# The same tasks in another order, in a delta-rule kernel followed by a gated feed-forward

## The chip, the core and the metric

The kernel runs on one core of a Trainium2 chip. The metric is the device time of one execution in microseconds (us); lower is better. Five engines of the core work side by side, each through its own instructions in a fixed order: TensorE (PE, matrix multiplication), VectorE (DVE), ScalarE (ACT), GpSimd (POOL) and SyncE (SP, which here only issues DMAs). An engine that comes to an instruction whose inputs are not ready waits, and everything behind it on that engine waits too. So the order of the instructions on each engine is a choice that decides what waits for what.

## The reference

Inputs q, k and v have the shape (4 batches, 8 heads, 768 tokens, 48); beta has one number for each token and head. Each head carries a 48x48 state through its tokens, and the result goes through a feed-forward of 384 to 2048 to 384:

```python
for t in range(S):
    kt, vt, bt = (k_n[:, :, t], v[:, :, t], beta[:, :, t, None])
    y[:, :, t] = np.einsum('bhd,bhde->bhe', q[:, :, t], state)
    v_old = np.einsum('bhde,bhd->bhe', state, kt)
    state = state + bt[:, :, :, None] * np.einsum('bhd,bhe->bhde', kt, vt - v_old)
...
h = x @ w_in          # x: (3072, 384), y with the heads side by side
g = h * np.cos(h)
return (g @ w_out).astype(np.float32)
```

k_n is k divided by its norm.

## The kernel before, in words

**Attention.** The 768 tokens are cut into 24 *units* of 32 tokens (n = 0 to 23); two units are a *pair* (m = 0 to 11). Within a unit the recurrence is solved at once: `turn(n)` and `gram(n)` (PE) make the products of the unit's keys and queries, `gram_keys` and `gram_queries` (DVE) scale and mask them, and `gram_put` and `gram_get` (SP) carry them through DRAM into the layout of the *inverse*. The inverse of pair m, `inv(m, 0)` to `inv(m, 6)` (lines 687 and 694), inverts triangular 32x32 blocks column by column, with a product and a subtraction for each column; it runs on GpSimd, only that of pair 0 (four steps, half size) on VectorE. `put(m)` and `get(n)` (SP) carry the result through DRAM back to where PE reads it as `zt` (`halves_z` in pair 0, with `get_odd(0)` issued on ScalarE's queue).

Then comes the chain from unit to unit: `state(n)` (PE, line 744), `old(n)` (ACT, 756), `right(n)` (DVE, 763), `solve(n)` (PE, 807 and 813; in pair 0 preceded by `solve_half`, `half_out`, `between` and `between_out`), `solve_out(n)` (DVE, 821), `update(n)` (PE, 834), `update_out(n)` (DVE, 842). `within(n)` (PE, 851), `within_out(n)` (ACT, 864) and `features(n)`, `features_out(n)` turn the unit's output into the input of the feed-forward.

**Feed-forward.** It works on pairs p = 0 to 11 of 256 rows. Pairs 0 and 1 use plain matmuls: `hidden(p, f)` (PE, 923), f = 0, 2, ..., 14, each with four steps after it: `turns` (ACT, 961), `rest` (DVE, 968), `cos` (ACT, 977), `gate` (DVE, 986), which together make h cos h. From pair 2 on, `layer(p, i)` (PE, 1105) uses sums of weights (`in_sums`, DVE, 1003 and 1007) and of inputs (`x_sum`, DVE) so that fewer products are needed; its `layer_copy` (ACT, 1121) and `merge` (DVE, 1007) join the pieces. The second matrix, `out(p, ...)` (PE, 1125 for pair 0, 1182 after), uses sums `right` of the weights and `left` of the gates (DVE, 1198) in the same way, and `collect` and `store` bring the result out. Two names are used twice: `right(n)` with one number is attention's, `right(x, e)` with two is a sum of weights.

**Weights.** The two matrices arrive as 64-bit floats and are narrowed on the chip in 28 pieces t: `weights(t)` (a DMA of 512 KB or 384 KB), `split(t)` (ACT, 448 and 450), `shift(t)` (DVE, 454 and 459), `add(t)` (POOL, 463). Pieces 0 to 11 are w_in: `hidden(p, 4)` and `hidden(p, 12)` need adds 0 to 8, `hidden(p, 6)` and `hidden(p, 14)` all of 0 to 11.

**What sets the order.** Each of these steps is a *task*, added with its engine and the tasks it needs. The class `Order` holds a list of numbers, `LINE`, each the number of a task, and `run` emits the tasks in that order. Each engine then executes its own tasks in the order in which they stand in `LINE`; the dependencies between engines become semaphores. Buffers are handed out in the same order too: a task that needs one of the eight large buffers "g" or of the three PSUM banks "h", or the single banks "two" and "kq", gets the one that was freed first, and waits for the last reader of what lay in it. So the order also decides which task's end sets a buffer free for which other task.

```python
for key in line:
    emit, deps, makes, uses = self.tasks[key]
    ...
        if tag in free:
            self.home = homes[t] = free[tag].pop(0)
    emit()
```

Of the kernel before, what the change touches and what calls it, by code (L numbers as in the profile page):

```python
# [53 lines left out]
0 1 2 3 4 5 6 2095 14 10 11 74 38 75 43 12 7 15 39 16 2099 40 44 13 41 45 46 77 48 99 17 47 18 49 19  # L54
20 78 2103 81 100 79 50 2107 102 2100 82 51 80 9 83 107 2111 2101 103 84 52 108 53 135 2108 2096 54
2102 104 55 105 2097 86 2104 2112 56 2115 37 57 109 2116 2119 160 2120 22 138 85 2109 110 42 2117
2098 2113 111 23 2105 2118 2123 2106 21 24 2121 2122 2114 112 25 139 2110 114 2124 140 26 2127 113
2125 2128 27 28 29 8 2131 136 30 31 2135 2129 32 33 142 34 59 141 193 2139 2126 58 143 2143 35 36
2132 2140 144 161 2136 115 60 2133 713 145 2144 76 146 61 62 63 64 2147 65 218 116 117 2148 66 2151
714 718 2141 2130 118 67 719 68 101 715 2137 70 69 2155 2134 164 720 723 119 2145 147 2142 2152 165  # L60
716 166 120 2149 2153 106 137 2138 2159 717 71 194 724 721 167 168 72 722 2156 121 169 2150 196 725
197 726 728 2157 2163 198 2154 2158 122 729 727 73 171 852 170 730 855 2160 2167 88 87 172 162 2171
89 200 733 2164 201 2161 731 738 853 199 90 91 732 856 734 2168 2169 92 2146 2165 735 743 736 737
251 2175 93 95 748 765 96 94 173 97 2170 174 124 2172 123 98 739 740 2179 2173 753 2162 202 741 742
276 859 744 2166 125 749 2183 745 750 203 205 204 126 781 2180 127 2181 746 163 2174 754 253 2176
309 747 786 128 129 175 782 2184 783 857 751 131 2182 2177 2187 254 752 176 132 2185 130 854 784
2188 2178 791 785 792 793 133 134 219 149 794 2189 222 787 177 788 796 2186 2191 334 858 795 223 150
2195 801 224 789 2192 178 2190 790 802 257 769 2193 179 2196 806 803 225 2199 797 2194 227 798 226
2197 148 799 804 755 2203 255 151 2198 2200 800 770 773 805 811 2201 152 2204 228 229 816 774 256
153 2202 258 2205 154 863 156 311 807 155 766 2206 157 756 812 181 195 312 757 808 259 759 180 158  # L70
868 182 809 861 183 869 860 184 864 871 185 280 813 760 220 279 186 159 862 188 814 810 777 865 189
815 761 822 367 762 190 281 187 872 817 221 191 260 261 818 262 207 230 866 763 758 231 819 820 771
772 780 821 232 824 873 282 315 192 778 316 827 208 283 764 828 874 876 875 830 877 285 832 233 886
768 234 888 767 887 825 823 889 826 892 890 235 775 893 252 878 867 879 895 894 901 891 317 833 903
896 284 882 209 834 829 236 902 897 898 899 880 237 263 904 835 911 836 900 905 906 881 907 206 909
313 287 286 885 210 908 779 211 914 910 912 212 288 213 915 913 214 838 215 925 916 289 917 216 239
918 919 338 840 238 831 841 920 240 884 921 392 290 776 922 241 242 923 924 277 217 842 931 243 926
927 244 314 246 932 425 928 929 843 247 245 933 930 934 248 844 291 837 249 935 936 883 845 846 870
940 337 318 941 942 292 937 319 320 310 839 265 943 944 946 848 849 938 945 939 952 250 947 339 293
948 949 850 966 950 951 953 960 340 369 996 965 997 961 341 847 954 962 321 373 342 999 343 955 1008  # L80
998 963 964 294 1009 956 968 957 1012 1000 971 958 1010 959 295 1014 972 1011 278 1013 370 1015 974
967 1016 1001 266 969 970 1025 374 1002 267 1017 1023 976 1018 1003 375 1019 264 1004 344 977 268
1024 1026 296 269 1020 978 1027 1028 851 1033 1007 345 979 1029 973 1021 1022 975 270 1030 272 980
395 1031 982 273 1036 1032 271 297 371 274 1034 450 1037 1035 984 298 346 985 372 1038 986 1039 299
1040 300 1041 983 1047 1042 1043 335 301 1044 302 987 1045 347 304 275 1046 1053 305 348 431 988 981
989 396 336 349 1048 1049 306 1054 1050 1055 307 1005 990 1006 992 483 1051 1052 1056 1062 1057 993
303 308 376 1063 1058 1064 1065 1059 994 1068 1060 1061 1066 377 378 1067 350 427 991 1074 1069 432
397 1087 1121 1075 1076 1118 1070 1090 1077 1078 1071 398 1119 1072 1079 323 1080 1073 1130 1081 995
1132 1082 1093 1083 1120 399 1131 1084 428 1085 1086 368 351 400 1088 1094 1134 1123 352 353 433 429
1136 1096 379 1089 1098 1133 1091 1092 1138 324 1135 1137 1145 1099 325 401 322 1139 453 1146 402  # L90
430 1122 1140 1126 326 1100 1141 1147 1101 1142 1125 1148 1102 327 1104 1143 403 1149 328 1150 1151
508 330 404 1129 1144 1124 393 489 454 331 1153 1154 1155 1152 1158 1106 329 1156 1095 1159 1097
1157 1160 1107 1161 1103 354 1108 1169 1162 355 1163 1109 1110 332 1128 405 1164 1165 1166 455 1167
# [1640 lines left out]
```

## Time and profile before

| what | value |
|---|---|
| median of 3 runs (lowest, highest) | 656.38 us (654.41, 659.73) |
| the profiled execution, its own time | 657.18 us |
| its span, first to last instruction | 655.2 us |
| mean granted TensorE clock in it | 0.990 |
| busy DVE, ACT, POOL in the span | 538.3, 356.6, 359.6 us |
| longest wait of GpSimd for a DMA of `gb` (inverse's input) | 16.4 us |
| longest wait of PE, for the DMA of `halves_z` | 16.5 us |
| DMA bytes | 59.40 MB, mean 91 GB/s |

The span is divided in the page into 40 slices of 16.4 us, with one digit for each engine: its busy share in tenths. In the views by time, a row has the start and the duration in us, the engine, the line, the operation, the tiles it writes and reads, their shape, and how many equal instructions were merged into it; in brackets stands the idle time before it and what ended that.

### The profile page before, as it was taken

Reading aid. Unit: us, or ns where it says so; the run is one execution under the profiler, and the core shown is the slowest. Engines: PE = TensorE matmul, PEld = TensorE weight load, DVE = VectorE, ACT = ScalarE, POOL = GpSimd, SP = SyncE. Lnnn points to the kernel's source line nnn. Section 1 sums busy time; section 2 is a strip of 40 time slices with the busy share of each in tenths; the row PEclk is TensorE's granted clock in tenths of the full one; section 3 lists DMA queues with packets and bytes.
Section 4 is the critical chain, followed back from the end, with each engine's and each line's share of the span. In section 5 each row is a group of like instructions: output and inputs, shape, how many; then the busy total and the mean of one; then the engine's idle time right before and its main releaser. Section 6 shows DMA issues by size and latency. Waiting matters only on the chain.

```text
span 655.2 us, 23573 instructions
## 1 busy us (share of the span) xinstructions
PE 594.3 (91%) x9724; PEld 552.3 (84%) x9724; DVE 538.3 (82%) x1098; ACT 356.6 (54%) x656; POOL 359.6 (55%) x735
## 2 busy tenths in 40 slices
PE   3326799999989999999999999999999999999997
PEld 3216688886788999998998998999999999989997
DVE  5684497979978998989988988989898879688782
ACT  3535386655346565556655565655665566556440
POOL 4258879877847748537718677178088284000000
PEclk9999699999999999999999999999999999999999
DMA  8887575466443554554454633553441513110001
GB/s 153 197 189 160 126 164 137 96 146 94 92 90 66 99 101 82 111 90 66 94 103 81 130 63 69 92 95 72 92 69 51 105 29 79 29 38 25 1 13 37
DMA packets 237070, 59.40 MB, mean 91 GB/s; under 512 B 228516, under 2 KB 231860, under 8 KB 236964
## 3 DMA queue, kind: packets, MB, share of 16 engines
q1 hardware_dynamic: 233956, 57.03, 44.3%
q8 instruction: 77, 1.26, 0.8%
q10 hardware_dynamic: 2752, 0.43, 0.5%
q0 software_dynamic: 256, 0.44, 0.3%
q14 instruction: 29, 0.24, 0.1%
HBM read 43.17 MB, written 14.68 MB: 88 GB/s over the span
## 4 chain that ended last, share of the span: by engine, by line
PE 59%; POOL 10%; DVE 7%; DMA 7%; ACT 7%; issue 5%; SPq 3%; POOLq 0%; ACTq 0%; DVEq 0%
PE p_h L1105 24%; PE p_out L1182 22%; POOL part L687 5%; POOL z L694 4%; ACT y L864 2%; PE p_s L834 2%; PE p_u L813 2%; PE p_g L577 2%; PE p_kq L851 2%; PE p_kq L744 2%; DVE p_h L1007 2%; PE p_o L1182 2%; DMA kp<-in_k_dram 1%; ACT g_ffn L1121 1%; POOL w_out L463 1%
## 5 line engine op out<-in xcount | busy, mean ns | idle before, releaser
L687 POOL TENSOR_TENSOR part<-z,gb 128x126 f32<-128x126 f32 (+22 forms) x341 | 140.3, 411 | 99.7 <-DMA gb<-g_dr 51.0
L694 POOL TENSOR_TENSOR z<-z,part 128x126 f32<-128x126 f32 (+22 forms) x341 | 145.6, 427 | 26.7
L1121 ACT COPY g_ffn<-p_h 128x512 f32<-128x512 f32 x140 | 79.2, 586 | 87.2 <-DVE p_h L1007 47.5
L1182 PE MATMUL p_out<-w_out,g_ffn 128*128 128x192 f32 x672 | 121.7, 329 | 1.0 <-DVE o L1232 1.0
L1182 PEld LDWEIGHTS p_out<-w_out,g_ffn 128*128 128x128 f32 x672 | 107.7, 190 | 2.5 <-DVE o L1232 1.5
L1007 DVE TENSOR_TENSOR p_h<-p_h,g_ffn 128x512 f32<-128x512 f32 x140 | 96.5, 694 | 15.7 <-PE p_h L1105 7.6
L961 ACT ACTIVATE turns<-p_h,quarter_turn 128x512 int32<-128x512 f32 x96 | 65.7, 687 | 63.9 <-DVE p_h L1007 50.0
L977 ACT ACTIVATE turns<-turns,halfpi 128x512 f32<-128x512 f32 x96 | 68.8, 722 | 55.0 <-DVE turns L968 54.1
L1182 PE MATMUL p_out<-w_sum,g_ffn 128*128 128x192 f32 x496 | 90.7, 331 | 0.7 <-DVE o L1232 0.6
L1105 PE MATMUL p_h<-x_sum,w_in 128*128 128x128 f32 x640 | 84.0, 278 | 1.3 <-ACT g_ffn L1121 0.7
L1182 PEld LDWEIGHTS p_out<-w_sum,g_ffn 128*128 128x128 f32 x496 | 79.5, 190 | 2.3 <-DVE o L1232 1.1
L1105 PEld LDWEIGHTS p_h<-x_sum,w_in 128*128 128x128 f32 x640 | 77.8, 192 | 3.8 <-ACT g_ffn L1121 2.4
L968 DVE SCALAR_TENSOR_TENSOR turns<-p_h,turns 128x512 f32<-128x512 f32 x96 | 65.5, 686 | 17.9 <-ACT turns L961 17.3
L986 DVE TENSOR_TENSOR g_ffn<-turns,p_h 128x512 f32<-128x512 f32 x86 | 58.6, 681 | 12.3 <-ACT turns L977 9.9
L1198 DVE TENSOR_TENSOR g_ffn<-g_ffn 128x512 f32<-128x512 f32 x88 | 61.9, 711 | 4.4 <-PE p_out L1182 4.3
L492 POOL TENSOR_TENSOR knrm<-ksum,halves 128x16 f32<-128x16 f32 (+1 forms) x14 | 36.6, 2615 | 40.5 <-DVE ksum L480 40.5
L1105 PE MATMUL p_h<-x_sum,in_sum 128*128 128x128 f32 x400 | 55.1, 281 | 2.1 <-DVE x_sum L1007 1.1
L864 ACT COPY y<-p_kq 32x384 f32<-32x384 f32 x96 | 45.1, 470 | 21.5 <-PE p_kq L851 17.7
L1105 PEld LDWEIGHTS p_h<-x_sum,in_sum 128*128 128x128 f32 x400 | 50.4, 194 | 4.2 <-DVE x_sum L1007 1.4
L923 PE MATMUL p_h<-x_ffn,w_in 128*128 128x128 f32 x384 | 47.7, 282 | 0.3 <-DVE g_ffn L986 0.3
L923 PEld LDWEIGHTS p_h<-x_ffn,w_in 128*128 128x128 f32 x384 | 45.7, 197 | 1.7 <-DVE g_ffn L986 0.6
L756 ACT COPY rhs<-p_kq 32x384 f32<-32x384 f32 x92 | 43.1, 468 | 6.3 <-PE p_kq L744 3.8
(124 smaller groups left out, 868.9 us busy)
## 6 DMA issues: line engine op xcount, KB each, us to landing
pairs<-in_moe_w_in_dram SPq DMA_DIRECT2D x12, 512.0 KB
pairs<-in_moe_w_out_dram SPq DMA_DIRECT2D x16, 384.0 KB
gb<-g_dr SPq DMA_DIRECT2D x22, 256.0 KB
vp<-in_v_dram SPq DMA_DIRECT2D x96, 48.0 KB
out_dram<-o SPq DMA_DIRECT2D x23, 192.0 KB
y_dr<-y_t SPq DMA_DIRECT2D x20, 192.0 KB
x_ffn<-y_dr SPq DMA_DIRECT2D x40, 96.0 KB
kp<-in_k_dram SPq DMA_DIRECT2D x128, 24.0 KB
```

The lines of the kernel that those rows point to most:

```text
L687: eng.tensor_tensor(out=part, in0=z[:, 0:rows, j, None].to_broadcast(shape), in1=a[:, j, None, j + 1 :].to_broadcast(shape), op=ALU.mult,)
L694: eng.tensor_tensor(out=behind, in0=behind, in1=part, op=ALU.subtract)
L923: nc.tensor.matmul(p_h[:, i], w_in[:, t, (4 * k + i) * 128 : (4 * k + i + 1) * 128], moved(p, t, unit), start=(t == 0), stop=(t == KT - 1),)
L961: nc.scalar.activation(turns[p, f], hidden_of(p, f), AF.Identity, bias=quarter_turn, scale=TURN)
L968: nc.vector.scalar_tensor_tensor(out=r, in0=hidden_of(p, f), scalar=TURN, in1=t, op0=ALU.mult, op1=ALU.subtract,)
L977: nc.scalar.activation(r, r, AF.Sin, bias=halfpi, scale=2.0 * math.pi)
L986: nc.vector.tensor_tensor(out=place(p, f), in0=step_of(rests.pop((p, f)), f), in1=step_of(hidden_of(p, f), f), op=ALU.mult,)
L1007: nc.vector.tensor_tensor(out=out, in0=one, in1=two, op=ALU.add if op == "add" else ALU.subtract)
L1105: nc.tensor.matmul(p_h[:, e], in_block(w)[:, e], form(p, x), start=first and e == 0, stop=True, skip_group_check=True,)
L1121: nc.scalar.copy(block(p, *CHAIN[i][3]), p_hs[p, BANK[i]])
L1182: nc.tensor.matmul(p_o, left(p, part, a)[:, e % 4], right(e, b), start=(e == 0), stop=(e == FT // 2 - 1), skip_group_check=True,)
L1198: nc.vector.tensor_tensor(out=left(p, s, to), in0=left(p, s, one), in1=left(p, s, two), op=op)
```

## The change

Only the list `LINE` differs. The first lines of both:

```diff
-0 1 2 3 4 5 6 2095 14 10 11 74 38 75 43 12 7 15 39 16 2099 40 44 13 41 45 46 77 48 99 17 47 18 49 19
-20 78 2103 81 100 79 50 2107 102 2100 82 51 80 9 83 107 2111 2101 103 84 52 108 53 135 2108 2096 54
...
+0 1 2 3 4 5 6 2095 10 14 11 12 74 38 15 43 39 7 40 13 75 16 44 17 41 2099 77 99 18 45 46 19 20 48 81
+47 78 49 2100 79 2103 100 102 2096 51 2097 50 103 80 2107 104 2101 107 9 52 2102 108 2111 82 53 135
...
```

The tasks, their costs and their dependencies are the same 2207; each engine gets the same instructions. By the change's description the new order was searched for (annealed) with GpSimd's steps taken to last longer where they overlap VectorE's sums. Read as tasks, the orders differ as follows in the stretches that the prediction speaks of (before, then after; in each engine's own order):

```
VectorE, start
  before: inv(0,0) inv(0,1) inv(0,2) inv(0,3) scale(1,1) shift(0) ...
  after:  inv(0,0) inv(0,1) scale(1,1) beta_home inv(0,2) inv(0,3) shift(2) ...
  before: sum(2,0) shift(7) between_out(0)
  after:  weigh(0) shift(5) scale(2,0) shift(6) shift(7) in_sums(4) between_out(0)
ScalarE, start
  before: inv_out(0) split(5) split(6) square(2,0) get_odd(0)
  after:  inv_out(0) split(3) split(4) square(2,0) get_odd(0) split(5) split(6)
  before: features_out(0) split(9) split(11) split(10) old(1)
  after:  features_out(0) split(9) old(1)
PE
  before: hidden(0,0) solve_half(1) between(1) solve(1) hidden(0,2) update(1)
  after:  hidden(0,0) hidden(0,2) solve_half(1) between(1) solve(1) update(1)
  before: turn(5) hidden(0,4) gram(5) features(1) hidden(0,6) state(2) turn(6) hidden(0,8)
  after:  turn(5) hidden(0,4) gram(5) features(1) state(2) hidden(0,6) turn(6) hidden(0,8)
  before: layer(2,9) out(1,3,0) layer(2,8) solve(6) layer(2,10)
  after:  solve(6) layer(2,9) layer(2,8) out(1,3,0) update(6) layer(2,10)
GpSimd
  before: norms(2) add(7) inv(1,0) (1,1) (1,2) add(8) (1,3) add(9) (1,4) add(11) (1,5) add(10) (1,6) add(13) norms(3)
  after:  norms(2) add(0,4,5,3,6,7) inv(1,0) ... (1,6) add(8) norms(3) add(9,10,12,15,11,14,13) inv(2,0)
  inside inverse 2 (pair 2): eight adds before, five after; inverse 3 is unbroken in both
VectorE and ScalarE after hidden(0,4)
  after, VectorE: gram_keys(5) shift(11) shift(15) gram_queries(5) rest(0,4) shift(14) gate(0,4) shift(16) gate(0,0) scale(3) rest(0,2)
  after, ScalarE: turns(0,4) within_out(1) split(15) split(14) cos(0,0) cos(0,4) split(16) eye(2) turns(0,2) cos(0,2) features_out(1)
SP
  before: put(1) gram_get(2) weights(18) get(2)          after: put(1) gram_put(5) weights(16) get(2) gram_get(2)
  before: put(2) weights(26) gram_put(7) get(4) weights(27) gram_get(3) blocks(8,1)
  after:  put(2) blocks(8,0) weights(26) get(4) gram_put(7) weights(27) blocks(8,1) gram_get(3)
  before: put(3) gram_put(8) get(6)                      after: put(3) gram_put(9) store(0,1) get(6)
```

In the new order `hidden(0,6)` gets the PSUM bank that `gate(0,4)` sets free (before: the one of `gate(0,0)`); `turn(6)` follows `features_out(1)` in the bank "two" in both.

## Prediction

> **What bounds the kernel now.** I read the page first, then the busy time by stretches, then the rows by time of PE and GpSimd where PE is not full. The page:
>
> ```profile
> span 655.2 us, 23573 instructions
> PE 594.3 (91%) x9724; PEld 552.3 (84%) x9724; DVE 538.3 (82%) x1098; ACT 356.6 (54%) x656; POOL 359.6 (55%) x735
> ...
> PE   3326799999989999999999999999999999999997
> ...
> POOL 4258879877847748537718677178088284000000
> ```
>
> PE is full from the sixth slice on; its work is unchanged, so an order can win or lose only what PE waits. That is 45 us in the first 100 and little after. Stretches (start:end, length, then busy PE, PEld, DVE, ACT, POOL, granted clock, DMA share, GB/s):
>
> ```profile
> 60.00:70.00 10.00, 6.95 (x207) 6.12 (x199) 3.53 (x5) 7.74 (x17) 8.98 (x17) 0.90 0.59 135
> 70.00:80.00 10.00, 7.96 (x171) 7.36 (x174) 4.61 (x8) 1.97 (x5) 8.61 (x17) 0.58 0.34 75
> 80.00:93.00 13.00, 11.29 (x286) 10.54 (x278) 11.31 (x20) 10.83 (x23) 10.28 (x18) 1.00 0.82 171
> 93.00:193.20 100.20, 95.43 (x1526) 81.19 (x1525) 87.84 (x158) 57.22 (x112) 82.03 (x142) 1.00 0.55 111
> 193.20:655.20 462.00, 450.34 (x6952) 428.66 (x6952) 390.86 (x792) 255.30 (x452) 218.69 (x502) 1.00 0.38 72
> ```
>
> Until 193 GpSimd is 80 to 90% busy: its inverses are the path there, and after 193 PE alone is. The rows of PE by time where that shows:
>
> ```profile
> 44.88 1.85 PE L773 MATMUL p_w<-vp,halves_z 32*32 32x48 f32 x64 [16.47 <-DMA halves_z<-z_dr]
> 67.79 1.83 PE L773 MATMUL p_w<-rhs,halves_z 32*32 32x48 f32 x64 [2.03 <-issue]
> 75.33 4.35 PE L923 MATMUL p_h<-x_ffn,w_in 128*128 128x128 f32 x24
> 82.50 2.84 PE L923 MATMUL p_h<-x_ffn,w_in 128*128 128x128 f32 x24
> ```
>
> ```profile
> 193.23 0.28 PE L813 MATMUL p_u<-rhs,zt 64*64 64x48 f32 x2 [1.28 <-DMA zt<-z_dr]
> 193.96 1.59 PE L813 MATMUL p_u<-rhs,zt 64*64 64x48 f32 x30 [0.45 <-DMA zt<-z_dr]
> ```
>
> The last pair is solve(6), waiting for the inverse of pair 3, which on GpSimd ends here (line 492 comes next, then inverse 4):
>
> ```profile
> 186.04 0.23 POOL L694 TENSOR_TENSOR z<-z,part 128x16 f32<-128x16 f32 x1
> 186.23 3.00 POOL L492 TENSOR_TENSOR knrm<-ksum,halves 128x16 f32<-128x16 f32 x1
> 197.54 0.24 POOL L687 TENSOR_TENSOR part<-z,gb 128x31 f32<-128x31 f32 x1 [8.31 <-DMA gb<-g_dr]
> ```
>
> From there GpSimd waits for DMAs instead of being waited for. So I compare three marks, solve(0), hidden(0,8) and solve(6), at 49.61, 92.78 and 193.23 before, and what PE still has to do after the last.
>
> **The change, part by part.** The order moves nearly every task; those that shift a mark are these.
>
> *To solve(0).* Two short tasks (scale(1,1) 1.0 us, beta_home 0.6) now stand inside the first inverse on VectorE: it ends at 34.1, not 32.5. But get_odd(0) no longer queues behind split(6), whose weights landed at 38.97; its DMAs were issued from 40.47 to 42.29 and set the 16.47 us wait. So solve_half(0) starts near 42.5, not 44.9. That gain is lost at between_out(0): behind weigh(0) VectorE now runs shift(5) 1.02, scale(2,0) 1.41, shift(6) 2.10, shift(7) 2.43, in_sums(4) 0.69, together 7.65, so between_out starts at 50.1 (before 49.0). Shifts take 1.0 alone and 2.0 to 2.4 beside GpSimd's adds; all short, it is 47.7. I take +0.7 (from -1.3 to +1.1), near the long rows, because the adds of these pieces run at that time.
>
> *To hidden(0,8).* Before, PE stood 2.03 us until old(1) got through behind three splits (3.5 us of ACT), and then ran at half clock (the 0.58). Now hidden(0,2) fills that hole. From the end of hidden(0,0), 66.5, PE has hidden(0,2) 2.85, then solve_half to turn(5), some 8.4 with their short waits at full clock: 77.7, where before it was 82.67. These 5 us are lost at once: hidden(0,4) needs add(8), which ran between steps of inverse 1 at 62.96 and now stands behind all seven. Inverse 1 starts near 50.8 (52.59 before): sum(2,0) now comes at 39, norms(2) takes 2.9 and the six adds up to add(7) 8.7. It takes 30.2 (sum of its seven steps), and add(8) 1.3: 82.3. PE stands 4.6 us, so I count hidden(0,4) at the half-clock 4.35 instead of 2.84: it ends at 86.6 (before 85.34).
>
> What is late next: features(1) uses the bank that gram_queries(5) frees, now behind shift(15), which waits for split(15) behind turns(0,4) 0.69 and within_out(1) 1.92: 4.9 us after hidden(0,4) ends (2.1 before). hidden(0,6) takes the bank of gate(0,4): turns, within_out, two splits 2.0, cos(0,0) 0.76, cos(0,4) 0.74, shift(14) on VectorE beside, gate 0.68: 7.4 after. turn(6) waits for features_out(1), which ScalarE now runs after cos(0,2), and that waits for rest(0,2) behind shift(16) 1.0, gate(0,0) 0.7, scale(3) 1.0 on VectorE: with rest 0.7, cos 0.7 and features_out 0.5, 12.0 after. turn(6) 1.1, so hidden(0,8) starts 13.1 after 86.6: 99.7, that is +6.9. Bounds: without half clock and with an inverse of 28.9 (the shortest of rows shown by time, pair 11's, 519.96 to 548.93) +3.7; with another half-clock stretch +8.4. add(11) (after norms(3) 3.1 and five adds) comes near 93, no later than the gate.
>
> *To solve(6).* From 92.78 to 193.23 PE took 100.4 us for tasks that, at the shortest row of each kind, need 88.7. Now layer(2,9), layer(2,8) and out(1,3,0) (0.89 + 0.89 + 1.30 = 3.1) stand behind solve(6): 85.6. I add 7 for changes of task, which cost 0.2 each (an x8 of line 1182 takes 1.30, after a small matmul 1.50): 99.7 + 92.6 = 192.3. The other arm: gram_get(2) now follows get(2) (1.9) but put(1) is 6 us earlier, so inverse 2 starts about as before (97.1); with three adds fewer inside it ends near 134 (137.8). gram_get(3) stands behind two more block loads (2.1 and 2.3), so inverse 3 starts near 149 (150.75), takes its 35.5, and get(6), past gram_put(9) and a store instead of gram_put(8), lands at 192. Both arms meet: solve(6) at 192.3, -0.9.
>
> *After solve(6).* PE has the 3.1 us more to do. Before, half clock followed the wait (x8 of line 1105 in 2.07 instead of 1.05, solve 1.6 instead of 0.7): 2 us, of which I take half back, -1.0, since PE and inverse arrive together. The remaining 17 units follow the same pattern with tasks a few places apart; I take 0, between -4 and +4, since PE's larger stalls there sum to some 9 us.
>
> Sum: -0.9 + 3.1 - 1.0 = +1.2 on the profiled execution's 657.18 (span 655.2 and 2.0 around it): 658.4. The median of the runs, 656.38, lies 0.8 below that execution: 657.6.
>
> **Two rules beside it.** The granted clock of 0.90 and 0.58 means half clock for 2 us before 70 and 8.4 after, some 10 us, though PE was 80% busy from 70 to 80. The Trainium skill (TensorE: Matmul & The Clock Gate, What's actually happening) has the full rate back after one busy window of about 3.4 us. By that rule a cold start costs at most half of 3.4, 1.7 us, and the cold rival below would give 657.6 + 2 x 1.7 - 1.5 = 659.5; this trace has both, a long stretch at 68 and a short one at 194, so its own rows set the price.
>
> The same 128x56 product on GpSimd takes 0.28 at 153.02 and 0.81 at 183.13. The Trainium skill (SBUF — State Buffer, Who interferes with whom) explains that by a port pair that GpSimd and a VectorE sum with two SBUF inputs lock against each other. The trace agrees in kind, and by that rule sums kept away from inverse 3 would win its whole stretch: the first rival.
>
> **Rivals.** *Faster: inverse 3 is no longer stretched.* It took 35.5 us with VectorE near full; pair 11's took 28.9. If it shrinks by 6.6, and hidden(0,8) starts by 93.5 so that PE can follow, solve(6) comes at 186: -7.2 + 3.1 - 2.0 = -6.1, 650.3. For it: the stretched rows above, and GpSimd's 82% before 193. Against it: VectorE's order keeps 12 in_sums and five left sums beside that inverse, as before. It decides from an end of the inverse before 180.
>
> *Slower: PE goes cold twice more.* Place: the waits at hidden(0,4) and features(1), 4 us each. The half-clock stretch from 68 to 78 cost 3.9 (hidden 1.5, solve_half 0.9, between 0.9, solve 0.6). Two of them, less the 1.5 counted, move solve(6) by 6.3: 663.9. It decides once add(8) ends after 82, so that both waits exceed 4 us. Against it: the half clock after 194 lasted for one x8 and solve(6) only.
>
> *No net effect: the order does not do what it was searched for.* GpSimd's steps are stretched as much as before, the late start is absorbed in waits that PE had anyway, and the 3.1 us in those saved: 656.4.
>
> *Later waits.* The order is worse after 200 by the +4 and more: 662.
>
> **How the numbers follow.** Forecast 0.40 (its own range 652 to 663), no net effect 0.12, faster 0.20, slower 0.20, later waits 0.08. The prediction is 657.6; the range reaches to both rivals and a little past, 649 to 667. 1% is 6.6 us, about what a measurement can tell from no change. Beyond it on the fast side lie half of the fast rival and the edge of the forecast: 0.12; on the slow side (over 662.9) most of the cold rival, half of the later waits and an edge of the forecast: 0.24; within: 0.64.
>
> **What would show it.** In the changed kernel's rows: solve(0) near 50; no wait before solve_half(1) and full clock from 68 to 77; PE idle 4 to 5 us before hidden(0,4), released by GpSimd's line 463; features(1) some 5 us after hidden(0,4); hidden(0,8) near 100; inverse 3 from 149 to 185; solve(6) at 190 to 194. Wrong if add(8) ends before 79, if hidden(0,8) starts before 95, or if inverse 3 ends before 181 or after 188; and if PE's waits after 200 differ by over 4 us.

## The result and the profile after

The changed kernel takes 661.81 us (median of nine runs, 658.86 to 663.11) against 654.41 us before (nine runs, 651.76 to 659.73): ratio 1.0099, 95% interval 1.0070 to 1.0129: slower by about 1%. Its profiled execution took 661.51 us, with a span of 659.7 us. That execution lies at its kernel's median; the one shown of before (657.18) turned out to lie 2.8 above the nine-run median of its kernel. So the two profiles that are read here differ by only 4.3 us, where the medians differ by 7.4.

From the page of the changed kernel (busy time, then GpSimd's line of slices):

```profile
PE 593.6 (90%) x9724; PEld 552.0 (84%) x9724; DVE 535.4 (81%) x1098; ACT 355.8 (54%) x656; POOL 350.3 (53%) x735
...
POOL 4266878886855848438638476286285382000000
```

GpSimd is busy 9.3 us less for the same instructions (before 359.6): its steps really are stretched less. PE's work is the same, and the span is 4.5 longer, so PE waits more. The stretches, with the same columns as before (start:end, length, busy PE, PEld, DVE, ACT, POOL, granted clock, DMA share, GB/s):

```profile
60.00:70.00 10.00, 9.22 (x138) 8.54 (x130) 2.78 (x5) 6.99 (x15) 8.51 (x20) 0.66 0.57 130
70.00:80.00 10.00, 6.80 (x308) 5.85 (x306) 7.15 (x12) 4.94 (x12) 8.59 (x19) 1.00 0.81 168
80.00:93.00 13.00, 5.75 (x84) 5.29 (x84) 2.69 (x6) 3.30 (x8) 10.87 (x17) 0.74 0.25 53
93.00:104.00 11.00, 7.93 (x95) 7.28 (x96) 10.07 (x19) 6.66 (x14) 7.91 (x13) 0.69 0.76 163
104.00:197.20 93.20, 91.36 (x1510) 78.24 (x1508) 77.43 (x142) 54.22 (x107) 72.09 (x130) 1.00 0.56 113
197.20:659.70 462.50, 450.92 (x6977) 428.94 (x6976) 394.57 (x801) 257.44 (x456) 212.67 (x502) 1.00 0.37 71
```

The stretch that was dense before, 80 to 93 (PE 11.29 busy), is now the emptiest: PE 5.75, VectorE 2.69, ScalarE 3.30, only GpSimd is at work. From 104 on PE is full. The rows of PE by time name the waits:

```profile
50.68 1.50 PE L807 MATMUL p_u<-u_half,halves_z 32*32 32x48 f32 x64 [5.90 <-DVE u_half L791]
...
79.11 0.61 PE L923 MATMUL p_h<-x_ffn,w_in 128*128 128x128 f32 x4
85.47 4.64 PE L923 MATMUL p_h<-x_ffn,w_in 128*128 128x128 f32 x20 [5.75 <-POOL w_in L463]
90.04 1.19 PE L577 MATMUL p_g<-kq_t 48*32 48x64 f32 x64
95.10 0.87 PE L872 MATMUL p_z<-consts,y 128*128 128x128 f32 x3 [3.87 <-DVE tt L611]
...
98.16 4.69 PE L923 MATMUL p_h<-x_ffn,w_in 128*128 128x128 f32 x24 [0.29 <-DVE g_ffn L986]
...
104.45 1.73 PE L923 MATMUL p_h<-x_ffn,w_in 128*128 128x128 f32 x14
...
197.18 1.13 PE L813 MATMUL p_u<-rhs,zt 64*64 64x48 f32 x32
```

hidden(0,4) issues four matmuls and stands 5.75 us for add(8) (line 463); features(1) then waits 3.87 behind gram_queries(5); hidden(0,6) runs at half clock (4.69, not 2.84); hidden(0,8) starts at 104.45, 11.7 later than before. solve(6), which before waited for the inverse of pair 3, waits for nothing and comes at 197.18, 4.0 later. GpSimd in the same time (the steps of the inverses left out):

```profile
49.64 1.66 POOL L463 TENSOR_TENSOR w_in<-w_in,pairs 128x512 uint32<-128x512 uint32 x1 [0.37 <-DVE w_in L459]
54.35 0.24 POOL L687 TENSOR_TENSOR part<-z,gb 128x31 f32<-128x31 f32 x1 [3.04 <-DMA vp<-in_v_dram]
...
84.14 1.28 POOL L463 TENSOR_TENSOR w_in<-w_in,pairs 128x512 uint32<-128x512 uint32 x1
...
94.70 1.01 POOL L463 TENSOR_TENSOR w_out<-w_out,pairs 128x384 uint32<-128x384 uint32 x1 [2.96 <-DVE w_out L459]
```

The second row is the one to learn from. Inverse 1's first step stands ready from 51.3, behind add(7), and starts at 54.35. It reads `gb`, which gram_get(1) brings; the name in the bracket, `vp`, is only the load beside it whose end the profile put the wait down to. On SP's queue (an issue row's duration is the time that the queue was held):

```profile
40.39 1.01 SPq L629 DMA_DIRECT2D g_dr<-g  x2
41.45 5.16 SPq L330 DMA_DIRECT2D vp<-in_v_dram  x4
47.13 0.35 SPq L440 DMA_DIRECT2D pairs<-in_moe_w_in_dram  x1
47.60 1.09 SPq L650 DMA_DIRECT2D gb<-g_dr  x2
48.74 2.06 SPq L330 DMA_DIRECT2D vp<-in_v_dram  x4
```

gram_get(1) (line 650) is issued at 47.60, behind v(2), which holds the queue for 5.16 us. Before, v(2) did not stand there, and it was issued at 44.55:

```profile
43.80 0.34 SPq L440 DMA_DIRECT2D pairs<-in_moe_w_in_dram  x1
44.55 1.09 SPq L650 DMA_DIRECT2D gb<-g_dr  x2
```

Inverse 1, add(8) behind it, and everything that follows come later by what this costs.

### The profile page after: what moved, and what is told of

It reads as the page before. It is cut to its first block, busy times and chain, and to the rows that moved or that the text cites. A ratio compares the mean times of both kernels' runs of the same rounds, so it can differ in the third digit from the quotient of the medians.

```text
span 659.7 us, 23572 instructions
## 1 busy us (share of the span) xinstructions
PE 593.6 (90%) x9724; PEld 552.0 (84%) x9724; DVE 535.4 (81%) x1098; ACT 355.8 (54%) x656; POOL 350.3 (53%) x735
## 4 chain that ended last, share of the span: by engine, by line
PE 71%; DVE 8%; ACT 7%; POOL 5%; DMA 3%; issue 3%; SPq 3%; DVEq 0%; ACTq 0%; POOLq 0%
PE p_h L1105 25%; PE p_out L1182 24%; PE p_h L923 5%; PE p_out L1125 3%; PE p_kq L744 3%; PE p_s L834 2%; PE p_kq L851 2%; ACT y L864 2%; PE p_u L813 2%; POOL z L694 2%; DVE p_h L1007 2%; POOL part L687 2%; PE p_g L577 2%; SPq L330 2%; DMA kp<-in_k_dram 2%
## 5 line engine op out<-in xcount | busy, mean ns | idle before, releaser
L687 POOL TENSOR_TENSOR part<-z,gb 128x126 f32<-128x126 f32 (+22 forms) x341 | 137.7, 404 | 116.2 <-DMA gb<-g_dr 76.9
L694 POOL TENSOR_TENSOR z<-z,part 128x126 f32<-128x126 f32 (+22 forms) x341 | 138.8, 407 | 26.7
L1007 DVE TENSOR_TENSOR p_h<-p_h,g_ffn 128x512 f32<-128x512 f32 x140 | 97.1, 695 | 20.9 <-PE p_h L1105 12.4
L968 DVE SCALAR_TENSOR_TENSOR turns<-p_h,turns 128x512 f32<-128x512 f32 x96 | 65.5, 684 | 13.1 <-ACT turns L961 12.4
L923 PE MATMUL p_h<-x_ffn,w_in 128*128 128x128 f32 x384 | 52.2, 300 | 6.0 <-POOL w_in L463 5.8
L923 PEld LDWEIGHTS p_h<-x_ffn,w_in 128*128 128x128 f32 x384 | 50.1, 213 | 7.5 <-POOL w_in L463 5.9
```

The costliest lines, as they stand in the source:

```text
L687: eng.tensor_tensor(out=part, in0=z[:, 0:rows, j, None].to_broadcast(shape), in1=a[:, j, None, j + 1 :].to_broadcast(shape), op=ALU.mult,)
L694: eng.tensor_tensor(out=behind, in0=behind, in1=part, op=ALU.subtract)
L923: nc.tensor.matmul(p_h[:, i], w_in[:, t, (4 * k + i) * 128 : (4 * k + i + 1) * 128], moved(p, t, unit), start=(t == 0), stop=(t == KT - 1),)
L968: nc.vector.scalar_tensor_tensor(out=r, in0=hidden_of(p, f), scalar=TURN, in1=t, op0=ALU.mult, op1=ALU.subtract,)
L1007: nc.vector.tensor_tensor(out=out, in0=one, in1=two, op=ALU.add if op == "add" else ALU.subtract)
```

## The experiments

All kernels below have the same 2207 tasks; only the order differs, except where said. Diffs are given as the tasks of one engine. "solve(6)" and the like are starts in the profiled execution of each kernel; "tail" is its span less solve(6). What some expectations call the landing of get(6) or gram_get is the end of its issue on SP. The table gathers all; ratios are against the kernel before, run beside them. A kernel's marks come from one execution, and some of these lie far from their kernel's median: the whole chain's 7.3 above it, the new head's 4.6 above, before's 2.8 and 2.9 above, and the old head's 2.0 below, the lowest of its twelve.

| kernel | inv. 1 | add(8) ends | hidden(0,8) | solve(3) | solve(6) | tail | profiled run | median (runs) | ratio, 95% |
|---|---|---|---|---|---|---|---|---|---|
| before | 52.6 | 64.3 | 92.8 | 116.0 | 193.2 | 462.0 | 657.18 | 654.41 (9) | |
| before, again | 51.2 | 62.9 | 93.1 | 116.0 | 192.9 | 462.6 | 657.41 | 654.51 (8) | 0.9993, 0.9967 to 1.0019 |
| changed | 54.3 | 85.4 | 104.4 | 127.6 | 197.2 | 462.5 | 661.51 | 661.81 (9) | 1.0099, 1.0070 to 1.0129 |
| old head | 50.7 | 63.1 | 87.3 | 111.5 | 190.2 | 462.6 | 654.60 | 656.56 (12) | 1.0024, 1.0005 to 1.0043 |
| new head | 56.2 | 87.2 | 106.4 | 129.7 | 205.1 | 462.7 | 669.62 | 665.07 (6) | 1.0155, 1.0122 to 1.0189 |
| add(8) earlier | 53.5 | 74.5 | 99.5 | 122.6 | 194.0 | 466.2 | 662.22 | 661.42 (6) | 1.0078, 1.0049 to 1.0107 |
| the same again | 55.1 | 76.2 | 100.4 | 123.4 | 193.3 | 462.1 | 657.48 | 658.59 (12) | 1.0056, 1.0036 to 1.0077 |
| PE kept busy | 53.8 | 84.8 | 102.8 | 125.9 | 196.9 | 463.6 | 662.28 | 661.69 (6) | 1.0088, 1.0063 to 1.0112 |
| behind hidden(0,4) | 53.1 | 83.8 | 101.7 | 127.6 | 197.2 | 462.6 | 661.57 | 661.57 (5) | 1.0117, 1.0093 to 1.0142 |
| gram_get(1) earlier | 50.6 | 81.3 | 99.3 | 122.5 | 192.1 | 462.5 | 656.42 | 656.66 (11) | 1.0049, 1.0029 to 1.0068 |
| GpSimd's hole | 54.2 | 84.9 | 103.8 | 126.8 | 196.4 | 462.2 | 660.35 | 660.44 (6) | 1.0115, 1.0086 to 1.0144 |
| three together | 50.7 | 72.5 | 99.8 | 123.0 | 193.5 | 462.1 | 657.60 | 657.02 (11) | 1.0052, 1.0030 to 1.0073 |
| whole chain | 51.4 | 75.0 | 97.1 | 128.9 | 202.2 | 464.2 | 668.33 | 661.00 (9) | 1.0094, 1.0060 to 1.0128 |
| old head, repaired | 51.2 | 63.1 | 92.7 | 115.6 | 194.1 | 462.3 | 658.12 | 657.47 (12) | 1.0041, 1.0020 to 1.0062 |

**Old head and new head.** Each order is cut behind solve(3) and joined to the rest of the other.

```diff
 old head:  LINE = [before, up to solve(3)] + [the rest as in the changed order]
 new head:  LINE = [changed, up to solve(3)] + [the rest as before]
```

> All tasks up to solve(3) in the old order, everything after in the new one. Theory A (the loss is made in the first 105 us and the later order is at least as good): hidden(0,8) back near 93, solve(3) near 116, and 651 to 655 us, so 0.995 to 1.00 of the kernel before. Rival B (the new order is worse throughout, among it the three tasks moved behind solve(6)): 657 to 660.

> All tasks up to solve(3) in the new order, everything after in the old one. Theory A: hidden(0,8) near 104 as in the changed kernel, and 661 to 664 us, at least as slow as it. Rival B: 656 to 658, since only the part before solve(3) is left of the loss and most of that is absorbed by 200 us.

The old head with the new rest: 656.56, so 5.2 of the changed kernel's 661.81 are gone, and the loss lies for the most part ahead of solve(3). It is not all of it: 1.0024 against before, an interval that leaves out 1, so the new rest from solve(3) on is no better than the old, rather 1 to 2 us worse in this join. The new head with the old rest is the slowest of all, 665.07. Neither theory's numbers were met: 656.56 lies between A's 651 to 655 and B's 657 to 660, and 665.07 lies a little above A's 661 to 664 and far from B's 656 to 658. The parts do not add up either: by the medians, the new head costs 5.2 us with the new rest and 10.7 with the old.

**add(8) earlier.** GpSimd alone: add(8) ahead of the sixth step of inverse 1.

```diff
-GpSimd: inv(1,4) inv(1,5) inv(1,6) add(8) norms(3)
+GpSimd: inv(1,4) add(8) inv(1,5) inv(1,6) norms(3)
```

> The changed kernel with one move: GpSimd does add(8) ahead of inv(1,5) instead of behind inv(1,6). Theory A (the wait for add(8) starts the loss): hidden(0,4) starts at 79 without a wait and runs at full clock, hidden(0,8) starts near 98, and 657 to 659 us. Rival C (the queues of VectorE and ScalarE behind hidden(0,4) decide, not its start): hidden(0,8) stays after 102, 661.

hidden(0,4) no longer stands for it, hidden(0,8) comes at 99.5 and solve(6) at 194.0, 3.2 earlier. But the median, 661.42, hardly moved, and the profiled execution lost what it had won at 490, in a place that the edit does not touch:

```profile
488.60 0.67 PE L851 MATMUL p_kq<-u,tt 32*32 32x48 f32 x49
490.89 0.38 PE L851 MATMUL p_kq<-u,tt 32*32 32x48 f32 x15 [1.63 <-issue]
491.21 2.93 PE L1182 MATMUL p_out<-w_sum,g_ffn 128*128 128x192 f32 x8
```

A wait for nothing that the profile names, in the middle of one group of matmuls, and half clock behind it (2.93 for an x8 that takes 1.57). So the same kernel was run again:

> The kernel with add(8) ahead of inverse 1's sixth step once more, unchanged. Its first profile had solve(6) at 194.0 (changed order 197.2), but also 3.5 us lost at 490.9 in matmuls that waited for nothing shown, and its median was 661.42. If that loss belongs to the execution and not to the order, this profile shows solve(23) 462.4 - 81 after solve(6) again, and the median comes out near 658.3. If the order itself loses them, the stall is at the same place and the median stays at 661.

```profile
487.24 0.80 PE L851 MATMUL p_kq<-u,tt 32*32 32x48 f32 x64
487.97 1.57 PE L1182 MATMUL p_out<-w_sum,g_ffn 128*128 128x192 f32 x8
```

No stall there, solve(6) at 193.3 and the usual tail: the stall belongs to the execution, not to the order. Whether the other runs of the first set had it is not shown. hidden(0,8) came at 99.5 and 100.4, so theory C, which wanted it after 102, fell. What add(8)'s place is worth is less clear: 0.4 us below the changed kernel by the first six runs, 3.2 by the twelve of the second set, and the intervals of the two ratios overlap each other and that of the changed kernel (1.0049 to 1.0107, 1.0036 to 1.0077, 1.0070 to 1.0129).

**PE kept busy.** The changed order, with 24 and 16 matmuls of no use put ahead of hidden(0,4)'s and features(1)'s first, into a PSUM bank that nothing reads yet. They are to fill PE's two waits, so that its clock is not halved behind them.

```diff
+        if (p, f) == (0, 4):
+            keep_busy(24)
...
+        if n == 1:
+            keep_busy(16)
```

> The changed kernel with 24 extra matmuls ahead of hidden(0,4) and 16 ahead of features(1), into a PSUM bank that is not yet in use, so that PE is busy through both waits; they add work and change no result. Theory D (the half clock after these waits is a large part of the loss): hidden(0,4) ends near 88 instead of 90.1, hidden(0,6) takes 2.9 instead of 4.7, hidden(0,8) starts near 101, and 659 to 660 us. Rival E (the chain over ScalarE, VectorE and GpSimd sets hidden(0,8) anyway): hidden(0,8) within 1 us of 104, 661 to 662.

The stretches 79 to 97 of this kernel, hidden(0,6), and solve(6):

```profile
79.00:84.00 5.00, 4.74 (x43) 4.74 (x44) 3.17 (x7) 1.20 (x4) 4.22 (x12) 1.00 0.61 134
84.00:97.00 13.00, 11.05 (x205) 10.38 (x204) 7.53 (x11) 7.75 (x15) 11.26 (x9) 0.98 0.58 118
```

```profile
96.50 4.51 PE L937 MATMUL p_h<-x_ffn,w_in 128*128 128x128 f32 x24 [1.47 <-DVE g_ffn L1000]
...
196.89 1.53 PE L813 MATMUL p_u<-rhs,zt 64*64 64x48 f32 x32 [0.98 <-DMA zt<-z_dr]
```

The clock stays full up to 96.4, through both waits. Then PE waits 1.47 for gate(0,4)'s bank, and hidden(0,6) runs at half clock all the same (4.51). So half clock in this stretch falls from twice 6.83 us to 3.41, not to nothing. hidden(0,8) comes 1.6 earlier, of which 0.6 is add(8) itself, and solve(3) 1.7 earlier; then solve(6) has to wait 0.98 for the inverse of pair 3, which is no earlier (it ends at 189.0, in the changed kernel at 188.6), and comes 0.3 earlier. The time is the same, 661.69, as theory E had it (661 to 662): with most of the half clock gone nothing is won, because the inverse's arm is only a little shorter than PE's.

**Behind hidden(0,4).** From here on two theories were set against each other: H, the late PE at hidden(0,8); G, the late start of inverse 2 on GpSimd.

```diff
-VectorE: gram_keys(5) shift(11) shift(15) gram_queries(5) rest(0,4) shift(14) gate(0,4)
+VectorE: gram_keys(5) gram_queries(5) rest(0,4) gate(0,4) shift(11) shift(15) shift(14)
-ScalarE: within_out(1) split(15) split(14) cos(0,0) cos(0,4) ... cos(0,2) features_out(1)
+ScalarE: within_out(1) cos(0,4) features_out(1) split(15) split(14) cos(0,0) ... cos(0,2)
```

> The changed order with PE's waits behind hidden(0,4) repaired and GpSimd's order untouched: on VectorE gram_queries(5), rest(0,4) and gate(0,4) stand directly behind gram_keys(5), ahead of shift(11) and shift(15); on ScalarE cos(0,4) and features_out(1) stand directly behind within_out(1), ahead of the splits. Two theories. H: the lost time is PE's, the late hidden(0,8) is what counts. G: it is GpSimd's, the start of inverse 2 is what counts (in the changed order 100.4, in the old head without PE's stalls 92.7; of these 7.7, 3.0 are idle before inverse 1, which waits for gram_get(1), and 3.0 idle before add(15), which waits for shift(15)). Here hidden(0,8) should start near 100 instead of 104.4, but shift(15) comes 2 to 3 us later, and inverse 2 then near 102. H expects solve(6) near 194 and 658 to 659.5. G expects solve(6) near 198 and 662 to 664, slower than the changed order, although PE is earlier.

H's 658 to 659.5 fell; G's time, 662 to 664, was nearly met, 661.57, as in the changed kernel. hidden(0,8) came 2.7 earlier, but 1.6 of that is an earlier add(8) in this execution (83.8, not 85.4), which the edit does not touch. Inverse 2 started at 99.4. PE's rows show how the 2.7 went:

```profile
97.13 3.86 PE L923 MATMUL p_h<-x_ffn,w_in 128*128 128x128 f32 x20 [3.42 <-POOL w_in L463]
...
108.56 1.23 PE L813 MATMUL p_u<-rhs,zt 64*64 64x48 f32 x32 [1.34 <-ACT w_out L448]
109.71 4.58 PE L923 MATMUL p_h<-x_ffn,w_in 128*128 128x128 f32 x24
...
127.65 1.23 PE L813 MATMUL p_u<-rhs,zt 64*64 64x48 f32 x32 [1.20 <-ACT ksq L475]
```

hidden(0,6) now waits 3.42 for the adds, whose shifts come later; solve(2) waits 1.34 (the bracket names a split, but what it reads, right(2), ended on VectorE at 108.35), and hidden(0,12) behind it runs at half clock (4.58 instead of 2.94). At solve(3), 127.65, nothing is left. Moving PE's wait is not removing it. That GpSimd's late adds are behind it is shown for the first of these waits, whose row names them, and not for the other two; the wait ahead of solve(3) is in the changed kernel as well (1.16).

**gram_get(1) earlier.** One task on SP; nothing else.

```diff
-SP: gram_put(3) gram_put(2) v(2) weights(8) gram_get(1) v(3)
+SP: gram_put(3) gram_put(2) gram_get(1) v(2) weights(8) v(3)
```

> The changed order with one task moved on SP: gram_get(1) ahead of v(2) and weights(8), which take SP from 41.5 to 47.5. Its DMA then lands near 48, and inverse 1 starts at 51.3, behind add(7), not at 54.3. Everything behind on GpSimd comes 3 earlier: add(8) ends near 82.4, inverse 2 starts near 97.4. G expects solve(6) near 194.2 and 658 to 659.5. H: hidden(0,8) comes at 101.4, and between 99.5 and 104.4 that made no difference in the two kernels before, so 661 to 662.

656.66: 5.1 below the changed kernel (4.7 by the means), the largest effect of any single move, and the intervals of the two ratios do not overlap (1.0029 to 1.0068, 1.0070 to 1.0129). SP and then GpSimd in this kernel:

```profile
39.79 1.01 SPq L629 DMA_DIRECT2D g_dr<-g  x2
45.23 1.09 SPq L650 DMA_DIRECT2D gb<-g_dr  x2
46.36 2.35 SPq L330 DMA_DIRECT2D vp<-in_v_dram  x4
```

```profile
49.00 1.66 POOL L463 TENSOR_TENSOR w_in<-w_in,pairs 128x512 uint32<-128x512 uint32 x1 [0.36 <-DVE w_in L459]
50.62 0.23 POOL L687 TENSOR_TENSOR part<-z,gb 128x31 f32<-128x31 f32 x1
```

gram_get(1) now waits only until its puts are through (45.23), and inverse 1 follows add(7) without a gap. On PE:

```profile
81.32 2.50 PE L923 MATMUL p_h<-x_ffn,w_in 128*128 128x128 f32 x20 [0.39 <-POOL w_in L463]
...
89.83 0.87 PE L872 MATMUL p_z<-consts,y 128*128 128x128 f32 x3 [5.22 <-DVE tt L611]
...
99.25 0.95 PE L923 MATMUL p_h<-x_ffn,w_in 128*128 128x128 f32 x7
...
192.11 1.14 PE L813 MATMUL p_u<-rhs,zt 64*64 64x48 f32 x32
```

The 5.75 us ahead of hidden(0,4) are 0.39, and the half clock behind them is gone; part of it comes back at features(1) (5.22 instead of 3.87). From hidden(0,8) on every mark is 5.1 to 5.2 earlier, to the end. H's number (661 to 662) fell, and G's sum (658 to 659.5) was too small: both arms hang on the start of inverse 1, PE's through add(8), the inverses' through GpSimd's queue, and so both move and neither holds the other back. The 0.5% by which this kernel is still slower than before, some 2 to 3 us, no run here explains.

**GpSimd's hole.** GpSimd alone; the 2.96 us in which it waits for shift(15).

```diff
-GpSimd: add(9) add(10) add(12) add(15) add(11) add(14) add(13) inv(2,0) add(16)
+GpSimd: add(9) add(10) add(12) add(13) add(11) add(15) inv(2,0) add(14) add(16)
```

> The changed order with GpSimd's order alone changed: behind norms(3) it is add 9, 10, 12, 13, 11, 15, inverse 2's first step, add 14 (before: 9, 10, 12, 15, 11, 14, 13, inverse 2). The 3.0 us in which GpSimd waits for shift(15) are filled, and inverse 2 starts near 97.8 (behind eye(2) on ScalarE) instead of 100.4. PE's waits stay: hidden(0,4) still ends at 90.1, hidden(0,8) still starts at 104.4. G expects solve(6) near 194.8 and 659 to 660. H expects no change, 661.5 to 662.

Inverse 2 starts 1.4 earlier (99.06; G wanted 97.8, but its first step still waits 3.21 for `gb`) and solve(6) 0.8. 660.44 is 1.4 below the changed kernel, yet the ratio, 1.0115, is no lower than that kernel's 1.0099: no effect on the time is shown. 660.44 lies between G's 659 to 660 and H's 661.5 to 662.

**Three together.** gram_get(1), add(8) and the hole in one kernel, and eye(2) ahead of split(15) on ScalarE.

> The changed order with the two idle stretches of GpSimd closed (gram_get(1) ahead of v(2), adds 12 and 13 ahead of 11 and 15, add 14 behind inverse 2's first step, eye(2) ahead of split(15) on ScalarE) and add(8) ahead of the sixth step of inverse 1. Inverse 1 starts at 51.3, hidden(0,4) waits for nothing, inverse 2 starts near 93.5. G expects solve(6) near 190.5 and 655 to 656.5, level with before. H expects hidden(0,8) near 97 and, since 99.5 brought 0.4 us only, 659 to 661.

657.02, no better than gram_get(1) alone, and between G's 655 to 656.5 and H's 659 to 661. hidden(0,4) waits for nothing, but features(1) waits 6.58 for gram_queries(5), behind shift(15), and hidden(0,8) is at 99.8 again. The gains do not add up: the next wait on VectorE takes their place.

**Whole chain.** The repair of all waits up to hidden(0,8), on four queues.

```diff
-GpSimd: inv(1,4) inv(1,5) inv(1,6) add(8) norms(3) add(9,10,12,15,11,14,13) inv(2,0) add(16)
+GpSimd: inv(1,4) add(8) inv(1,5) inv(1,6) add(9,10,11) norms(3) add(12,13) inv(2,0) add(15,14,16)
-VectorE: update_out(1) shift(12,10,13) gram_keys(5) shift(11) shift(15) gram_queries(5) rest(0,4) ...
+VectorE: update_out(1) shift(10,11) rest(0,2) gate(0,0) shift(12) gram_keys(5) gram_queries(5) rest(0,4) gate(0,4) gate(0,2) shift(13,15,14) right(2) ...
-ScalarE: split(13) turn_out(5) turns(0,4) within_out(1) split(15) ...
+ScalarE: split(13) cos(0,0) turns(0,2) turn_out(5) turns(0,4) within_out(1) cos(0,4) cos(0,2) features_out(1) old(2) eye(2) split(15) ...
-SP: gram_put(2) v(2) weights(8) gram_get(1)
+SP: gram_put(2) gram_get(1) v(2) weights(8)
```

> The changed order with the whole chain to hidden(0,8) repaired. SP: gram_get(1) ahead of v(2). GpSimd: add(8) ahead of inverse 1's sixth step; behind the seventh add 9, 10, 11, norms(3), 12, 13, inverse 2's first step, 15, 14. VectorE: shift(10), shift(11), rest(0,2), gate(0,0) ahead of gram_keys(5), and gram_queries(5), rest(0,4), gate(0,4), gate(0,2) ahead of shift(13), shift(15), shift(14). ScalarE: cos(0,0), turns(0,2) ahead of turn_out(5), and cos(0,4), cos(0,2), features_out(1), old(2), eye(2) ahead of the splits. Theory H (the time is the start of hidden(0,8), and then solve(3), plus a tail of PE that never waits): hidden(0,8) near 92, solve(3) near 116, and solve(6) at 187 to 188, where the inverse of pair 3 would now come last (inverse 2 starts near 91, and get(6) landed 94.3 after that start in the kernel with gram_get(1) moved); with the tail of 462.4 and 1.9 around the span 651.5 to 653, below both kernels. If the tail does not follow, and waits show up in it, 655 to 658.

A miss: 661.00. The profiled execution is the slowest of the nine (668.33), so its rows explain that execution; whether the others had the same waits is not shown. hidden(0,8) did come at 97.1, but two adds had been put behind inverse 2's first step, and that step waits for gram_get(2), whose second transfer landed at 98.62 (the bracket names a neighbour again). GpSimd, VectorE and PE:

```profile
98.78 0.42 POOL L687 TENSOR_TENSOR part<-z,gb 128x31 f32<-128x31 f32 x1 [4.29 <-ACT turns L961]
...
102.05 2.93 POOL L463 TENSOR_TENSOR w_out<-w_out,pairs 128x384 uint32<-128x384 uint32 x3
```

```profile
104.05 1.34 DVE L1211 TENSOR_TENSOR w_sum<-w_out 128x384 f32<-128x384 f32 x1 [3.21 <-POOL w_out L463]
```

```profile
108.46 2.01 PE L813 MATMUL p_u<-rhs,zt 64*64 64x48 f32 x32 [5.83 <-ACT kq_t L554]
```

right(1,0) holds VectorE for these adds until 104.05; behind it rest(0,6) is late, behind that on ScalarE cos(0,6) and turn_out(6) (line 554), and PE stands 5.83 us at solve(2). It is the same mistake as the changed order's add(8), one inverse later.

**Before, again.** The kernel before, unchanged, for a second profile.

> The kernel before, unchanged, for a second profile. In the first one PE lost 1.87 at 52.80, 2.03 at 67.79 and 1.18 at 72.53 waiting for nothing shown, and that execution lay 2.8 above the median of nine. The kernel with the old head started hidden(0,8) at 87.3 and solve(6) at 190.2, against 92.8 and 193.2. If those stalls belong to that execution, this profile has hidden(0,8) at 87 to 88, solve(6) near 190.3 and a span near 652.3; if the order makes them, 92 to 93 and 193 again.

The stalls are there again, at the same instructions, and hidden(0,8) is at 93.1, so they do not belong to one odd execution. But they are two, not three. PE in this profile, with one row of VectorE:

```profile
52.67 0.54 PE L807 MATMUL p_u<-u_half,halves_z 32*32 32x48 f32 x14 [0.23 <-issue]
...
72.50 0.70 PE L773 MATMUL p_v<-u_half,halves_z 32*32 32x48 f32 x22 [1.73 <-issue]
```

```profile
67.02 0.64 DVE L763 TENSOR_TENSOR rhs<-vp,rhs 128x384 f32<-128x384 f32 x1 [1.95 <-ACT rhs L756]
```

The 2.03 us before 67.79, which the expectation counts among them, are an ordinary wait that the row does not name: solve_half(1) reads what right(1) writes on VectorE, and starts 0.10 us after that ends, here (67.66, 67.76) as in the first profile, in the old head and in its repaired form. The other two stand inside groups of 64 equal matmuls: 1.87 and 1.18 us in the first profile, 0.23 and 1.73 in this one. In the kernel with the old head, which executes the same tasks in the same order up to there, both groups are whole:

```profile
48.04 1.54 PE L807 MATMUL p_u<-u_half,halves_z 32*32 32x48 f32 x64 [0.74 <-DVE u_half L791]
...
66.83 0.88 PE L773 MATMUL p_v<-u_half,halves_z 32*32 32x48 f32 x64 [0.57 <-ACT u_half L783]
```

Three of four profiles with this head have the stalls (hidden(0,8) at 92.7 to 93.1), one has not (87.3). Whether they set the time of an execution is not shown: the eight times here leave a gap between 654.7 and 657.4, but the 26 of the same kernel measured beside them run from 652.1 to 658.0 without one, and both profiles of the kernel before have the stalls, so there is none without them to compare.

The traces do say what the stalls go with. The DMA queue that the profiles call "instruction" brings 77 packets of 16 KB in every profile, about one for each 256 of PE's matmuls and weight loads. In the first profile with add(8) earlier one of them is all that moves on the DMA queues from 488 to 491, around the stall that ends at 490.89:

```profile
DMA packets 1, 0.02 MB, mean 5 GB/s; under 512 B 0, under 2 KB 0, under 8 KB 0
...
q8 instruction: 1, 0.02, 2.0%
```

The stalls lie whole multiples of 256 PE instructions apart, and the seven of them end 1.25 to 1.52 us after the end of such a packet (here 489.55; in the first profile of before 51.38, with the matmuls going on at 52.80). With one packet counted for each 256, no such stretch of any profile starts less than 1.23 us after its packet's end. In the old head the packet in question ends at 47.54, before PE needs it. So PE stands there until its next instructions have come. Why they come late in one execution and not in another, no run shows.

**Old head, repaired.** The experiments suggested a version below both kernels: the old head with the new rest, and the waits that its profile shows between solve(3) and solve(6) taken out.

```diff
-SP: put(2) blocks(8,0) weights(26) get(4) gram_put(7) weights(27) blocks(8,1) gram_get(3)
+SP: put(2) gram_put(7) gram_get(3) weights(26) get(4) weights(27) blocks(8,0) blocks(8,1)
-GpSimd: add(25) add(26) add(27) inv(3,0) inv(3,1)
+GpSimd: add(25) inv(3,0) add(26) add(27) inv(3,1)
-VectorE: solve_out(3) rest(1,0) sum(4,0) gate(0,14) update_out(3) ... shift(25) gram_keys(7)
+VectorE: solve_out(3) update_out(3) rest(1,0) gate(0,14) ... gram_keys(7) shift(24) ... shift(25)
-ScalarE: cos(0,12) square(4,0) turns(1,0) ... within_out(3) ... turns(1,8) eye(3)
+ScalarE: cos(0,12) turns(1,0) ... within_out(3) square(4,0) ... eye(3) ... turns(1,8)
```

> The old order through solve(3) and the new one behind it, as in the first splice (hidden(0,8) 87.3, solve(6) 190.2, tail 462.6, profiled span 652.8), with the places repaired at which that profile shows waits up to solve(6). SP: behind put(2) gram_put(7) and gram_get(3) come first, then weights(26), get(4), weights(27) and the two blocks loads (before: gram_get(3) last). GpSimd: inverse 3's first step ahead of add(26) and add(27). VectorE: update_out(3) ahead of rest(1,0), which let PE wait 3.58 at turn(7), and gram_keys(7) ahead of shift(24). ScalarE: square(4,0), which waits for its tokens until 120, behind within_out(3), and eye(3) earlier. If solve(6) is set by whichever comes last of PE's own work and the inverse of pair 3: turn(7) near 121 instead of 124.6 and no half clock behind it, inverse 3 from about 140 instead of 147.0, get(6) landing near 182, solve(6) at 185 to 187, and with an unchanged tail 649 to 651.5, below both kernels. If the waits only move on (to add(26), add(27) or get(4)), solve(6) stays at 189 to 191 and the time at 653.5 to 656.

Not so: 657.47, like the first splice (656.56), above before, and past both branches of the expectation. The profiled execution had the stalls in its head; inverse 3 did start 2.9 earlier and solve(6) no longer waited for it, but new waits at features(3) (2.52) and hidden(1,6) (1.17, then 5.49 at half clock instead of 2.94) ate the rest. No version tried here beats the kernel before.

## Why the prediction was right or wrong

The time, 661.8, lies in the range and 4.2 above the 657.6 forecast. The mechanism was right (the head comes later because hidden(0,4) waits for add(8), PE is full from hidden(0,8) on), the size was not: the forecast change was +1.2 us, the measured one +7.4. That the time is in the range owes something to a range 18 us wide and to a base that was 2.0 too high (656.38 of three runs, 654.41 of nine), which makes the miss look smaller than it is. The number alone does not choose the mechanism, either: 661.8 is nearer to the 662 of the later waits and the 663.9 of the cold rival than to 657.6; the experiments choose it. By steps:

*solve(0)*: the time was right, in part by luck. between_out(0) was put at 50.1 and ran at 50.1; solve(0) at 50.68 (50.3). But solve_half(0) began at 40.72, not 42.5, and the tasks on VectorE behind weigh(0) took 9.4 us, not 7.65: scale(2,0) alone took 4.84 (forecast 1.41).

*Clock from 70 to 80*: right, 1.00 instead of 0.58. From 60 to 70 it is 0.66, which the forecast did not have: hidden(0,0) and hidden(0,2) took 7.86 together, and turn(5) ended at 79.3, not 77.7. It cost nothing, since hidden(0,4) waited anyway.

*hidden(0,4) waits for add(8)*: the mechanism was right, the size not, and here the forecast fails: "Inverse 1 starts near 50.8". Only GpSimd's own queue was counted. Its inputs come through SP, and gram_get(1) there stands behind v(2); inverse 1 started at 54.35: add(7) ended 0.5 later than forecast, at 51.30, and this wait added 3.04. It lasted 29.8 to the end of its last step (30.2 forecast), so add(8) ended at 85.4 instead of 82.3. That moving gram_get(1) alone puts inverse 1 at 50.6, add(8)'s end at 81.3, hidden(0,8) at 99.3 (forecast 99.7) and solve(6) at 192.1 (forecast 192.3) shows that this was the missing term. That 99.3 and 192.1 come so near is partly luck: in that kernel hidden(0,4) ran at full clock and ended at 83.8, 2.8 before the forecast, and hidden(0,8) came 15.4 behind it instead of 13.1, so the steps behind it held in their sum and not one by one.

*The chain behind hidden(0,4)*: right for features(1), 5.0 after its end (4.9); a little short for hidden(0,6), 8.0 (7.4), and hidden(0,8), 14.3 (13.1). Together with 3.1 for add(8) and 0.3 for a longer hidden(0,4) these make the 4.7 by which hidden(0,8) came later than forecast.

*From hidden(0,8) to solve(6)*: right for PE's arm. 85.6 of work and 7 for changes of task, 92.6; it took 92.7. "Both arms meet" was nearly so: in the changed kernel PE is last, with PE kept busy the inverse is, by 0.98. The inverses' arm was too early in the forecast: inverse 2 began at 100.42 (97.1), inverse 3 at 154.44 (149) and ended at 188.6. The prediction had named an end after 188 as a sign of being wrong, and solve(6) at 190 to 194 as one of being right; by 0.6 and 3.2 us both spoke against it. Both go back to the late inverse 1: with gram_get(1) alone moved inverse 3 runs from 149.36 to 183.5.

*After solve(6)*: +2.1 forecast (3.1 more work, 1.0 of half clock back), +0.5 measured: the tail is 462.5 against 462.0. Before, solve(6) was followed by 2 us of half clock; those went wholly, not by half, and some half a us more. The "0, between -4 and +4" for the rest held: eleven of the fourteen profiles have a tail of 462.0 to 462.7, whatever comes ahead of it (463.6 with PE kept busy, 464.2 in the whole chain, 466.2 with the stall at 490).

*The profiled execution against the median*: 0.8 was taken off for it, after three runs. By the runs since it is 2.7 or so, while the changed kernel's profile lies at its median. This is 1.1 of the 4.2; the sum at solve(6) is +4.9, the tail -1.6, the time around the span -0.2.

The rivals. *Inverse 3 not stretched* fell: its end was at 188.6, and it took 34.2 instead of 35.5. The order did shorten GpSimd's work, by 9.3 us in all, but 6.0 of that lies behind solve(6) (212.67 busy instead of 218.69), where PE is full. *PE cold twice more* came true as a place and not as a price: add(8) did end after 82, one wait exceeded its mark of 4 us (5.75) and the other just missed it (3.87), and half clock followed each, 2 x 0.26 x 13 = 6.8 us in one stretch and 2 x 0.31 x 11 = 6.8 in the next; but with most of it gone (3.41 of the 13.7 us left) the time was the same (661.69). The Trainium skill (TensorE: Matmul & The Clock Gate, What's actually happening) gives the full rate after at least one busy window of about 3.4 us. The trace agrees with that length as the unit and not with one as the number: each of these stretches lasted 6.83 us, two of them, and one stretch of the first profile of before 10.24, three. *No net effect* fell with the interval above 1. *Later waits* fell with the tail.

## What to carry to other kernels

When an order is changed, follow each input of the stage on the path through every queue that brings it, the DMA queue too: here one task, v(2), that holds SP for 5.16 us ahead of a small transfer cost 5.1 of the 7.4 us lost, and no view of the compute engines names it. Before a profile is used as the base of a sum, look at whether its execution is a typical one: the two profiles read here differ by 4.3 us where the medians differ by 7.4. And a wait taken out by hand mostly shows up at the next late task; of the repairs tried here, only the one at the common source of both arms kept all of its gain.

## What the runs showed of the hardware

PE can stand for 0.2 to 1.9 us inside a group of equal matmuls, with no wait that the rows name ("issue"). In this head it happens between the same two instructions (after 50 of 64 and after 42 of 64) in three of four profiles, and at 490 in one of two profiles of another kernel. All seven of these stalls end 1.25 to 1.52 us after a packet of 16 KB on the queue called "instruction" (x3_add8: 489.55 and 490.89), and they lie multiples of 256 PE instructions apart. Why a packet is late is open.

Not every "issue" in a bracket is such a stall: solve_half(1) starts 0.10 us after right(1) ends on VectorE in all four profiles with this head (67.66 and 67.76 in one), and its bracket says "issue" as well.

The granted clock can halve behind a short wait and then stays so for longer than the wait: 6.83 us behind each of two waits of 5.75 and 3.87 us here, 3.41 behind the stall of 1.63 us at 490. No wait length decides it in these runs: the old head has a wait of 1.53 us at 94.4 with no half clock behind it, before one of 1.28 at 193.2 with it. In the records of the fourteen profiles half clock lasts 3.41, 6.83, 10.24, 13.65 or, at the start, 40.96 us: multiples of 3.41.

SP's queue is held by the issue of a DMA, and not in proportion to its bytes: 2.06 to 5.16 us by four loads of 48 KB, 0.35 by one of 512 KB, 1.09 by two of 256 KB.
